# Turning the centroids earlier, and copying the fourth head on VectorE, in a fused clustered-attention and expert kernel

## The chip, the cores and the metric

One core of one Trainium2 chip. The metric is the time of the whole kernel on the device, in microseconds (us), lower is better. Places in a trace are us from the start of its span; the span is about 1.8 us shorter than the time.

Engine names in the profile: PE is TensorE's matmuls, PEld its weight loads, DVE is VectorE, ACT is ScalarE, POOL is GpSimd, SP is SyncE. L242 is line 242 of the kernel. In experiments that add or take lines, the same statement has a number a little higher or lower.

## The reference, cut to what matters

```python
# q, k, v: (4 batches, 8 heads, 768, 64) float32; centroids: (8 heads, 16, 64)
c_n = centroids / (norm(centroids) + 1e-06)
q_assign = argmax(einsum('bhsd,hcd->bhsc', q_n, c_n))     # 16 clusters a head
k_assign = argmax(einsum('bhsd,hcd->bhsc', k_n, c_n))
mask = q_assign[:, :, :, None] == k_assign[:, :, None, :]
attn_out = softmax(where(mask, q @ k.T / 8, -1e9)) @ v
# then, on the 3072 x 512 result: four experts, weighted by domain_probs
out = sum over e of  p[:, e] * (relu(x @ w1[e]) @ w2[e])
```

Keys and queries are first scored against the centroids of their head. Everything else waits for the first of these scores.

## The kernel before

In the trace of this kernel each engine runs the stretch below in the order of the statements: TensorE starts the twelve transposes of the keys from 4.63 to 6.42 us, that of the centroids at 6.53 and those of the queries from 6.81; ScalarE's four copies start from 5.54 to 6.82 and its cast at 7.20; VectorE lays out the centroids from 6.84 and copies the queries from 7.50. The first keys are turned (transposed) head by head on TensorE into PSUM and copied from there to SBUF (`all`, shown as tile `t`). The centroids are turned too and laid out block by block in `bdc`. A score is a matmul of `bdc` with the turned heads:

```python
def lay_centroids():
    pt = bank("misc")
    nc.tensor.matmul(pt[:, :128], cn2, ident, is_transpose=True)             # L185
    for r in range(2):
        dve(bdc[r * D:(r + 1) * D, :, r * CL:(r + 1) * CL],                  # L187
            pt[r * D:(r + 1) * D, :128].rearrange("p (h c) -> p h c", c=CL))
...
def turn(self, y, copy, shared=False):     # three transposes per head of the first keys
    ...
            nc.tensor.matmul(tp[:, c0:c0 + 128], raw[...], ident, is_transpose=True)   # L242
    ...
    copy(t32, tp[:, :m * w])                                                 # L252
...
def scores(self, copy):
    sc = self.bank()
    for j in range(HG):                    # four heads, four strips of 32 columns
        nc.tensor.matmul(sc[32 * j:32 * j + 32, :self.w], bdc[:, self.g * HG + j, :],
                         self.t32s[j // self.m][:, c0:c0 + self.w], ...)     # L267
    copy(self.scs[:, :self.w], sc[:, :self.w])                               # L271
...
for j in range(HG):                        # HG = 4
    k0.turn(j, act)                        # act: a copy on ScalarE
lay_centroids()
qa.turn(0, dve, True)                      # the first queries, copied by VectorE
k0.cast(0, 0, act)
k0.scores(act)
qa.scores(act)
```

Much later, in the experts, ScalarE applies the Relu that TensorE's second matmul reads.

```python
ht = moe.tile([128, 512], BF16, name="hT")
nc.scalar.activation(ht, ph, ACT.Relu)                                       # L745
...
nc.tensor.matmul(po, hT[f // per][:, c0:c0 + 128], W2[e][:, f, c], ...)      # L758
```

The softmax here doesn't subtract the row's maximum and nothing guards it: scores larger than these inputs give would overflow.

## Time and profile before

| | before |
|---|---|
| time, median of the first 3 runs | 472.22 us (472.22 to 472.25) |
| TensorE busy | 463.2 of 470.4 us |
| ScalarE, VectorE busy | 59%, 48% |
| key scores (L267) start, end | 7.58, 8.43 us |
| query scores (L267) start | 8.25 us |

TensorE is busy nearly throughout, so the time is its busy time plus the few gaps in it.

### The profile page before, as it was taken

What the parts mean: (1) busy time and instruction counts of PE and PEld (TensorE: products, weight loads), DVE (VectorE), ACT (ScalarE), POOL (GpSimd) and SP (SyncE); (2) the same over time, 40 slices, a digit from 0 to 9 for tenths busy, and PEclk for the clock granted to TensorE, in tenths of its full rate; (3) what the DMA queues carried; (4) which work ended last, traced back from release to release, by engine and by line L of the source; (5) the groups of instructions that cost most, each with busy time, mean ns of one, the idle gap of its engine ahead of it and who ended that gap; (6) DMA issues with size and microseconds to landing.
All of it is one profiled execution on the core that took longest, in us unless ns stands there. A gap on an engine that the chain in (4) does not pass through costs nothing.

```text
span 470.4 us, 11349 instructions
## 1 busy us (share of the span) xinstructions
PE 463.2 (98%) x4505; PEld 329.1 (70%) x4505; DVE 227.4 (48%) x554; ACT 276.9 (59%) x502; POOL 194.8 (41%) x301
## 2 busy tenths in 40 slices
PE   8999999999999999999999999999999999999996
PEld 5778777767767766777776667766766666667665
DVE  5964723542325563321234463523778767674112
ACT  5767675445655655566565656656665675664342
POOL 5936779275355593450433942000233232230000
PEclk9999999999999999999999999999999999999999
DMA  8999966996645941503666844220100100100101
GB/s 277 262 211 339 216 99 120 236 127 182 144 68 127 182 114 32 144 18 61 169 123 127 133 106 151 71 75 11 52 13 8 54 11 10 33 29 11 46 2 45
DMA packets 82381, 49.85 MB, mean 106 GB/s; under 512 B 57944, under 2 KB 77080, under 8 KB 82328
## 3 DMA queue, kind: packets, MB, share of 16 engines
q1 hardware_dynamic: 73080, 39.80, 35.1%
q0 software_dynamic: 8576, 9.25, 11.0%
q8 instruction: 35, 0.57, 0.5%
q14 instruction: 18, 0.15, 0.1%
q10 hardware_dynamic: 672, 0.08, 0.1%
HBM read 37.31 MB, written 6.30 MB: 93 GB/s over the span
## 4 chain that ended last, share of the span: by engine, by line
PE 95%; DVE 2%; DMA 1%; issue 0%; ACT 0%; SPq 0%; ACTq 0%
PE ps_mo L739 36%; PE ps_mo L758 35%; PE ps_s L649 9%; PE ps_av L676 7%; PE ps_s L562 1%; DMA kf<-oht 1%; PE ps_misc L562 1%; PE ps_s L87 1%; PE ps_mo L406 1%; PE ps_mo L242 1%; PE ps_misc L406 1%; DVE kf L315 1%; PE ps_misc L242 1%; PE ps_mo L267 0%; PE ps_misc L267 0%; DVE oh L287 0%
## 5 line engine op out<-in xcount | busy, mean ns | idle before, releaser
L655 ACT ACTIVATE at<-ps_s 128x512 bf16<-128x512 f32 x252 | 147.6, 596 | 115.5 <-PE ps_s L649 100.1
L739 PE MATMUL ps_mo<-xT,w1b 128*128 128x256 bf16 (+1 forms) x1664 | 195.9, 264 | 0.0
L758 PE MATMUL ps_mo<-w2b,hT 128*128 128x512 bf16 (+2 forms) x784 | 190.0, 375 | 0.0
L739 PEld LDWEIGHTS <-w1b 128*128 128x128 bf16 x1664 | 146.1, 98 | 24.8 <-issue 1.2
L745 ACT ACTIVATE hT<-ps_mo 128x512 bf16<-128x512 f32 x192 | 114.7, 598 | 60.5 <-PE ps_mo L739 57.7
L767 DVE SCALAR_TENSOR_TENSOR oacc<-ps_mo,psb,oacc 128x512 f32<-128x512 f32 (+1 forms) x74 | 54.3, 734 | 125.3 <-PE ps_mo L758 125.1
L758 PEld LDWEIGHTS <-hT 128*128 128x128 bf16 x784 | 66.9, 98 | 57.8 <-issue 3.1
L649 PE MATMUL ps_s<-qf,kf 80*128 80x256 bf16 (+1 forms) x456 | 82.7, 267 | 0.8 <-ACT at L655 0.4
L676 PEld LDWEIGHTS <-at 128*128 128x128 bf16 x1152 | 69.9, 97 | 15.3 <-issue 1.7
L676 PE MATMUL ps_av<-vx,at 128*128 128x65 bf16 x1152 | 80.3, 193 | 0.0
L662 POOL TENSOR_TENSOR at<-at,same 128x512 bf16<-128x512 bf16 x24 | 28.2, 1177 | 98.5 <-ACT at L655 83.0
L649 PEld LDWEIGHTS <-kf 80*128 80x128 bf16 x456 | 42.1, 98 | 20.6 <-issue 1.4
L380 POOL COPY t<-t 128x768 uint16<-128x768 uint16 x40 | 44.3, 1127 | 0.0
L579 DVE TENSOR_SCALAR same<-qf,late 128x256 bf16<-128x256 bf16 x144 | 39.0, 323 | 0.0
L662 DVE TENSOR_TENSOR at<-at,same 128x512 bf16<-128x512 bf16 x48 | 21.6, 450 | 25.9 <-ACT at L655 25.9
L364 POOL COPY h<-raw 128x768 uint16<-128x768 uint16 x24 | 20.3, 864 | 30.4 <-DMA raw<-in_k_dram 16.7
L361 POOL COPY h<-raw 128x768 uint16<-128x768 uint16 x16 | 13.1, 829 | 39.3 <-DMA raw<-in_q_dram 32.3
L765 DVE TENSOR_SCALAR oacc<-ps_mo,psb 128x512 f32<-128x512 f32 x18 | 13.5, 748 | 27.0 <-PE ps_mo L758 27.0
L683 DVE RECIPROCAL zr<-ps_av 128x4 f32<-128x4 f32 (+1 forms) x50 | 8.9, 178 | 33.3 <-PE ps_av L676 33.2
L336 POOL DMA_DIRECT2D qf<-oht x40 | 20.4, 519 | 7.5 <-DVE oht L313 3.9
L422 POOL COPY st<-sct 128x384 uint16<-128x384 uint16 x16 | 11.0, 736 | 28.8 <-DMA sct<-scs 28.8
L685 DVE TENSOR_TENSOR xn<-ps_av,zr 128x256 bf16<-128x256 f32 (+1 forms) x50 | 20.7, 414 | 1.7
(130 smaller groups left out, 263.2 us busy)
## 6 DMA issues: line engine op xcount, KB each, us to landing
raw<-in_v_dram SPq DMA_DIRECT2D x8, 768.0 KB, 5.4
out_dram<-oacc SPq DMA_DIRECT2D x23, 256.0 KB, 2.0
raw<-in_k_dram SPq DMA_DIRECT2D x7, 768.0 KB, 7.5
raw<-in_q_dram SPq DMA_DIRECT2D x6, 768.0 KB, 5.7
w1b<-in_moe_w_dram POOLq DMA_DIRECT2D x4, 1024.0 KB, 12.3
w2b<-in_moe_w_dram POOLq DMA_DIRECT2D x4, 1024.0 KB, 17.6
qf<-nos SPq DMA_DIRECT2D x2, 768.0 KB, 5.2
xT<-xn SPq DMA_TRANSPOSE x80, 2.4
```

Source lines behind the costliest of these rows:

```text
L336: (nc.gpsimd if self.b or self.i0 and self.g else nc.sync).dma_start(out=self.rows(slice(D, D + CL), j, r), in_=self.oht[p0:p0 + CL, :self.w])
L380: pool(self.all[:, y * w:(y + 1) * w].bitcast(U16)[:, z::2], self.t16[:, (2 * z + y) * w:(2 * z + y + 1) * w])
L579: nc.vector.tensor_scalar(same[:, x * 256:(x + 1) * 256], clusters(b)[:, g, w, k // 2, k % 2, :], key_nos[b % 2][:, g, 8 * i + 4 * (k // 2 ...
L649: nc.tensor.matmul(sp[:, x * n:(x + 1) * n], KF[b % 2][:K, h, r, i * 128:(i + 1) * 128], QF[b % 2][:K, h, rs[0]:rs[-1] + 1, w * 128:(w + 1 ...
L655: nc.scalar.activation(at, sp, ACT.Exp, scale=scale)
L662: (nc.gpsimd if n4 in POOL_STEPS else nc.vector).tensor_tensor(at, at, same_cluster(b, w, cur), op=ALU.mult)
L676: nc.tensor.matmul(av[:, h % 2, m, :], at[:, c0:c0 + 128], VX[b % 2][:, h, 2 * i + r, :], start=(first and x == 0 and m == 0), stop=(last ...
L685: nc.vector.tensor_tensor(xn[:, :nr].rearrange("p i j d -> p j i d"), av[:, :, :, :D], zr.broadcast_to([128, 2, nr, D]), op=ALU.mult)
L739: nc.tensor.matmul(ph[:, x * n:(x + 1) * n], W1[e][:, i, (f + x) * 128:(f + x + 1) * 128], xT[:, i, :], start=(i == 0), stop=(i == ND - 1))
L745: nc.scalar.activation(ht, ph, ACT.Relu)
L758: nc.tensor.matmul(po, hT[f // per][:, c0:c0 + 128], W2[e][:, f, c], start=(f == 0), stop=(f == NF - 1))
L767: nc.vector.scalar_tensor_tensor(oacc[:, c], po, pap, oacc[:, c], op0=ALU.mult, op1=ALU.add)
```

## The change

Its intent: the layout of the centroids should no longer come after everything else the first scores need, and ScalarE should no longer have four copies in a row ahead of them.

```diff
-    for j in range(HG):
+    for j in (0, 1):
         k0.turn(j, act)
     lay_centroids()
+    k0.turn(2, act)
+    k0.turn(3, dve)
     qa.turn(0, dve, True)
```

No instruction is added or removed in total. The centroid transpose takes TensorE's seventh place instead of the thirteenth, and one copy goes from ScalarE's stream to VectorE's.

## The prediction

> **What bounds the kernel now.** I read the page first (busy shares, slices), then the list of who waited for whom on TensorE, then the chain of waits in order of time, and last the timelines of TensorE, ScalarE and VectorE over the first eleven microseconds, because everything that the change touches happens there.
>
> From the page:
>
> ```profile
> PE 463.2 (98%) x4505; PEld 329.1 (70%) x4505; DVE 227.4 (48%) x554; ACT 276.9 (59%) x502; POOL 194.8 (41%) x301
> PE   8999999999999999999999999999999999999996
> PE 95%; DVE 2%; DMA 1%; issue 0%; ACT 0%; SPq 0%; ACTq 0%
> ```
>
> TensorE is busy for 463.2 of 470.4 us and carries 95% of the chain. The change alters none of its work (the same thirteen transposes, one of them in another place), so it can only take idle time away from it. All of the span outside its busy time is 7.2 us, and some of that is the start-up and the tail that nothing here touches. The waits of TensorE, longest first, are few:
>
> ```profile
> PE ps_misc L296 <- DVE oh L287: 0.6, 2, 0.4
> PE ps_s L649 <- ACT at L655: 0.4, 2, 0.3
> PE ps_mo L276 <- ACT scs L271: 0.4, 1, 0.4
> PE ps_s L649 <- DMA kf<-oht: 0.3, 1, 0.3
> PE ps_mo L296 <- DVE oh L287: 0.2, 1, 0.2
> ```
>
> Each column is the total, the count and the longest in us. They all lie in the first 28 us (the row for 60 to 470 us of the table by stretches shows no wait worth a line). So a head start won at the beginning reaches the end undiminished, if it survives every gate up to about 28 us; nothing later gives it back.
>
> Now the stretch that is edited. This is the chain of waits there (start, length, what):
>
> ```profile
> 4.79 1.58 PE ps_mo L242 x9
> 6.37 0.33 PE ps_s L242 x3
> 6.70 0.11 PE ps_misc L185
> 6.81 0.66 PE ps_av L242 x4
> 7.47 0.11 issue
> 7.58 0.95 PE ps_mo L267 x8
> 8.55 0.49 ACT scs L271
> 9.08 0.56 PE ps_mo L276 x3
> 9.66 0.56 DVE mx L284
> ```
>
> The reader should see the 0.11 us "issue" between 7.47 and 7.58: the scores of the first keys (L267) could have begun when the transposes of the queries ended, and something else held them. The timelines say what:
>
> ```profile
> 6.81 0.42 PEld L242 LDWEIGHTS ps_av<-ident,raw 128*128 128x128 f32 x4 [0.24 <-DMA raw<-in_q_dram]
> 6.82 0.50 ACT L252 COPY t<-ps_s 128x384 f32<-128x384 f32 x1
> 6.84 0.59 DVE L187 COPY bdc<-ps_misc 64x128 f32<-64x128 f32 x2 [1.26 <-PE ps_misc L185]
> 7.50 0.69 DVE L252 COPY t32q<-ps_av 128x512 f32<-128x512 f32 x1
> 7.55 0.19 PEld L267 LDWEIGHTS ps_mo<-t,bdc 128*32 128x32 f32 x8 [0.32 <-ACT t L252]
> 8.25 0.16 PEld L267 LDWEIGHTS ps_av<-t32q,bdc 128*32 128x32 f32 x8 [0.51 <-DVE t32q L252]
> ```
>
> Two things must be there for these scores: the fourth head's copy (ScalarE, 6.82 + 0.50 = 7.32) and the laid-out centroids (VectorE, 6.84 + 0.59 = 7.43). The list names ScalarE as releaser, but the centroids were ready 0.11 us after it. They, not the copy, were the later one.
>
> [...] at 59% and 48% neither is short of time, and both sit in front of L267. [...] The trace has 0.56 us (the L252 copy of a head on VectorE at 13.16) and 0.48 to 0.50 us, so VectorE is the slower place by some 0.06 to 0.08 us[...]. [...] transposes 0.21 us apart at about 5 us and 0.11 us apart after 6 us.
>
> **The change part by part.**
>
> 1. The centroid transpose (L185) goes from slot 13 of the thirteen transposes to slot 7. Its input is ready: the second scaling of the centroids ends at 5.06 + 0.25 = 5.31. Single transposes in the trace start at 6.10, 6.21, 6.31, 6.42 and 6.53 (slots 9 to 13), and slot 6 at 5.72, so slot 7 starts at about 5.88 and ends 0.27 later, at 6.15. VectorE, idle since 5.58, then copies the centroids from about 6.19 to 6.78 instead of 6.84 to 7.43. That gate opens 0.65 us earlier.
>
> 2. Heads three and four are transposed one slot later, 0.11 us. The third head's copy on ScalarE moves from 6.45 to about 6.56, and ends near 7.04. Nobody waits for that.
>
> 3. The fourth head's copy goes to VectorE. Its last transpose takes slot 13 and ends at 6.81, so the copy runs 6.84 + 0.56 = 7.40. On ScalarE it ended at 7.32. This gate gets 0.08 us later.
>
> 4. ScalarE loses 0.37 us of serial work (its copies start 0.37 us apart), and its first cast, from 7.20, starts near 6.9. Nothing on the chain reads that cast before 12.66.
>
> 5. The query copy on VectorE waits for the query transposes, and these for a DMA that lands at about 6.8, whatever stands before them on TensorE. It starts at 7.50 as before, since VectorE is free at 7.40. So the query scores still start at 8.25.
>
> Sum: the last input of the key scores was ready at 7.43 and will be at 7.40: 0.03 us. What may be added is the handover. From 7.43 to the weight load at 7.55 took 0.12 us, where other releases in this trace take 0.05 to 0.06 (the query copy ends at 8.19 and its load starts at 8.25). The first score matmul waited on two engines at once; after the change the build has it wait for inputs long present, and only the fourth for VectorE. The four heads use separate 32-column strips and run side by side (four start within 0.02 us, four second passes 0.32 us later), so the fourth alone sets the end. If its weights load at 7.40 + 0.06 = 7.46, the gain is 0.09 us. Total: 0.03 to 0.09 us.
>
> From there: ScalarE's score copy (8.55), the transpose back (9.08), max and one-hot on VectorE all move with it. The transposes of the next keys at 9.79 wait for a DMA and don't move, but the one-hot transpose waits 0.23 us behind them for VectorE, so up to about 0.2 us still passes. From 12.06 to 19 VectorE is the chain, nearly without gaps, and moves as a block. Then comes
>
> ```profile
> 20.01 4.60 DMA kf<-oht
> 24.75 0.22 PE ps_s L649
> ```
>
> a small transfer that lands 4.6 us after its issue, amid weight loads that keep all 16 queues full. TensorE waits 0.27 us for it. If its latency stays 4.6 us, the gain passes; its four copies took 4.6 to 4.8.
>
> My expectation is a gain of about 0.08 us, 472.22 to 472.14; I round to 472.1.
>
> **Rivals.**
>
> A: ScalarE was the true gate, as the releaser column says, with its four copies in a row. Then relieving it would free the scores by up to the end of the query transposes: their last starts at 7.20, so the scores could start at 7.31, a gain of 0.24 to 0.27 us, and 471.95. For it: the column. Against: the copy ended at 7.32, 0.23 us before the load, and in the new order the fourth head is on VectorE until 7.40, so even then the fourth strip can't start at 7.31.
>
> B: VectorE becomes the bound. Its 0.56 us copy stands ahead of the query copy; if it starts late (centroid copies behind a late L185)[...], the query copy and all after it slip by 0.1 to 0.2 us: 472.3 to 472.4. Against: VectorE is idle from 5.58, and there is 0.10 us between 7.40 and 7.50.
>
> C: the small transfer hides it: it lands when the full queues let it, not 4.6 us after its issue. Then the wait at 24.75 grows by what was won, and the time stays 472.2, or moves by its own scatter of 0.2 us either way.
>
> **Range and chances.** The central case is 472.1; A and C reach down to about 471.9, B and C up to 472.4. The three runs before differ by 0.03 us, but another session or chip may add a few tenths, so I take 471.7 to 472.5. A change of 2% is 9.4 us, more than all the idle time of TensorE, so faster by that is out of reach, and slower would need a new wait where I see none: faster 0.005, same 0.985, slower 0.01.
>
> **What would show it.** In the changed profile: the centroid copies end before 6.9 on VectorE; the fourth head's copy runs there at about 6.84 to 7.40; the weight loads of L267 for the fourth head at 7.46 to 7.55; ScalarE's score copy at 8.43 to 8.52; the one-hot transpose of 10.89 earlier by the same; the transfer of 20.01 likewise, and TensorE's step at 24.75. I am wrong if the score copy starts at 8.3 or before (rival A), if the query copy starts after 7.55 (B), or if the shift seen at 19 us is gone at 25 us (C).

## The result, and the profile after

| | before | after |
|---|---|---|
| median of 4 runs | 472.24 us (472.22 to 472.28) | 472.37 us (472.29 to 472.40) |

The ratio is 1.0002, with an interval of 0.9985 to 1.002: the same at 2%. (Ratios here are the mean time of one kernel's runs over that of the other's of the same rounds, so not quite the ratio of the medians quoted.) Still, all four runs of the changed kernel lie above all four of the kernel before, by 0.13 us in the median, where a gain of 0.08 was predicted.

The busy times after, from the page:

```profile
span 470.5 us, 11349 instructions
PE 463.2 (98%) x4505; PEld 328.6 (70%) x4505; DVE 227.9 (48%) x555; ACT 276.4 (59%) x501; POOL 194.4 (41%) x301
```

TensorE's busy time is unchanged; one instruction went from ACT (502 to 501) to DVE (554 to 555). The chain of waits at the start, after (start, length, what):

```profile
1.76 4.91 DMA raw<-in_q_dram
6.67 0.04 issue
6.72 0.66 PE ps_av L242 x4
7.38 0.90 PE ps_mo L267 x8
...
8.30 0.49 ACT scs L271
...
8.83 0.56 PE ps_mo L276 x3
...
9.42 0.56 DVE mx L284
```

and three lines of VectorE's timeline there:

```profile
5.59 0.59 DVE L187 COPY bdc<-ps_misc 64x128 f32<-64x128 f32 x2
6.57 0.56 DVE L252 COPY t<-ps_s 128x384 f32<-128x384 f32 x1 [0.39 <-PE ps_s L242]
7.41 0.69 DVE L252 COPY t32q<-ps_av 128x512 f32<-128x512 f32 x1 [0.28 <-PE ps_av L242]
```

The gap before the scores is gone, and the copy of the scores starts at 8.30 instead of 8.55. The chain now begins with the load of the first queries (landed 6.67), no longer with the transposes of the keys. So the start of this trace is 0.25 us earlier, which is more than predicted; the experiments show below that the clock did most of it. Down the line, the chain at 20 us:

```profile
19.76 4.67 DMA kf<-oht
24.43 0.14 issue
24.56 0.22 PE ps_s L649
```

24.56 instead of 24.75: the lead of 0.25 us became 0.19 in the small transfer (4.67 against 4.60 us). The transfer runs while the weights load: from 20.00 to 24.60 us of the kernel before, the packets of the weights' queue alone took 112.5% of the span of the 16 DMA engines. When TensorE's matmuls of both traces are set side by side in program order, the changed kernel is ahead by 0.191 us (median) from 45 to 95 us and **behind by 0.083 us** from 102 to 170, and it stays so to the end. Something takes 0.274 us at one place. The chain there, first the kernel before:

```profile
98.99 0.12 PE ps_av L676 x4
99.12 1.34 PE ps_mo L739 x24
100.46 0.89 PE ps_mo L758 x4
```

and after:

```profile
98.84 0.61 ACT at L655
99.44 0.30 issue
99.75 0.61 ACT hT L745
100.36 0.05 issue
100.40 1.04 PE ps_mo L758 x4
```

Before, TensorE runs through (but for about 0.02 us, see the account below). After, it waits for a Relu of ScalarE, and the Relu starts 0.30 us after the exponential in front of it, in a stretch that the view calls "issue": time in which the engine waited for nothing that the profile shows. In the kernel before, the same Relu starts 0.03 us after that exponential (99.627 to 99.658 us).

Counting the records of ScalarE's stream in order, from zero and with its event waits and DMA issues, gives a lead (places, start to end in us):

```
before                                     after
190  99.029- 99.627  exponential           189  98.838- 99.435  exponential
191  99.599- 99.616  wait for an event     190  99.408- 99.425  wait for an event
192  99.658-100.255  Relu                  191  99.749-100.346  Relu
```

The removed copy moved every later ScalarE instruction up by one place. Elsewhere too the changed kernel has stretches of 0.31 to 0.34 us, right after an event wait, in which ScalarE stands idle. They end at 175.36, 243.12 and 449.97 us, and these are places 319, 447 and 831: all, like 191, are 63 more than a multiple of 128. The kernel before has one such gap, at 313.26 us, place 575, again 63 more than a multiple of 128. This gave the theory to test:

- **Theory (fetch).** ScalarE's sequencer pays about 0.3 us once in 128 instructions (the name is my guess at the cause). It costs nothing where ScalarE waits for another engine anyway, as just ahead of place 191 before, where the exponential on place 190 waited 2.35 us for TensorE; and it costs TensorE 0.27 us where a Relu with no slack stands there.
- **Rivals.** The gap is chance; or it belongs to the fourth copy on VectorE or to the new timing of the first 30 us; or any extra ScalarE instruction helps.

### The profile page after: what moved, and what is told of

Same layout as the page of the kernel before. It is cut to its first block, busy times and chain, and to the rows that moved or that the text cites. A ratio compares the mean times of both kernels' runs of the same rounds, so it can differ in the third digit from the quotient of the medians.

```text
span 470.5 us, 11349 instructions
## 1 busy us (share of the span) xinstructions
PE 463.2 (98%) x4505; PEld 328.6 (70%) x4505; DVE 227.9 (48%) x555; ACT 276.4 (59%) x501; POOL 194.4 (41%) x301
## 4 chain that ended last, share of the span: by engine, by line
PE 94%; DVE 2%; DMA 2%; ACT 0%; issue 0%; SPq 0%; ACTq 0%
PE ps_mo L758 35%; PE ps_mo L739 35%; PE ps_s L649 9%; PE ps_av L676 7%; PE ps_s L562 1%; DMA raw<-in_q_dram 1%; DMA kf<-oht 1%; PE ps_misc L562 1%; PE ps_mo L406 1%; PE ps_misc L406 1%; DVE kf L315 1%; PE ps_misc L242 1%; PE ps_mo L267 0%; PE ps_misc L267 0%; DVE oh L287 0%; DVE mx L284 0%
## 5 line engine op out<-in xcount | busy, mean ns | idle before, releaser
L739 PE MATMUL ps_mo<-xT,w1b 128*128 128x256 bf16 (+1 forms) x1664 | 195.9, 264 | 0.0
L758 PE MATMUL ps_mo<-w2b,hT 128*128 128x512 bf16 (+2 forms) x784 | 190.0, 375 | 0.1
L739 PEld LDWEIGHTS <-w1b 128*128 128x128 bf16 x1664 | 146.1, 98 | 24.7 <-issue 1.2
L758 PEld LDWEIGHTS <-hT 128*128 128x128 bf16 x784 | 66.9, 98 | 58.1 <-issue 3.1
```

The costliest lines, as they stand in the source:

```text
L739: nc.tensor.matmul(ph[:, x * n:(x + 1) * n], W1[e][:, i, (f + x) * 128:(f + x + 1) * 128], xT[:, i, :], start=(i == 0), stop=(i == ND - 1))
```

## The experiments

In every trace I measured the same two things: TensorE's shift against the first trace of the kernel before, as the median from 45 to 95 us and from 102 to 170 us, and their difference, the step at 100.3 us.

### One instruction more, early (after_pad1, after_pad1_again)

```diff
     nc.scalar.activation(warm, blank[:, :1], ACT.Exp)
+    pad = consts.tile([128, 1], F32, name="pad")
+    for x in range(1):
+        nc.scalar.activation(pad[:, x:x + 1], blank[:, :1], ACT.Exp)
```

> The changed kernel with one more ScalarE instruction, a 128x1 exponential right after the warming one, in time where ScalarE idles. Fetch theory (ScalarE's sequencer pays some 0.3 us at every 128th instruction, at place 63 of each 128, and the change, by taking one instruction out, put a Relu that TensorE waits for on place 191): the extra instruction puts the stream back where it stood before the change, the 0.31 us gap before the Relu at 99.7 us is gone, TensorE keeps its lead of 0.19 us past 100 us, and the time is 472.05 to 472.15. Rival (the loss at 100 us is chance in a DMA or comes of the fourth copy on VectorE): the time stays at 472.3 to 472.4.

> after_pad1 once more, beside the changed kernel in the same job. Fetch theory: no gap at place 191, and 0.25 to 0.45 us below the changed kernel in the mean; with the first query load landing near 6.35 us, 471.6; near 6.7 us, 472.05 to 472.15.

Measured: medians 472.12 (471.62 to 472.80) and 472.19 us (471.52 to 472.61), ratio to the kernel before 0.9994 both times. The step at 100.3 us is 0.000 and 0.001 us; the Relu is on place 192, 0.03 us behind its exponential. The spread of single runs is wider than expected (below).

### The changed kernel again (again_after, third_after)

> The changed kernel unaltered. Fetch theory: the gap of about 0.3 us stands again before the same Relu (ScalarE instruction 191, near 99.7 us), and the time is 472.29 to 472.40. Chance: the gap is gone or elsewhere, and the time of the runs without it is near 472.1. Also to see when the full clock is granted (3.98 us in the first profile, against 5.81 in the kernel before), and when the scores of the first keys start then (7.30 us in the first).

> The changed kernel once more, beside after_pad1_again. Gap of about 0.31 us before the Relu on place 191; 472.3 to 472.4 with the query load landing near 6.7 us, 471.9 to 472.0 with it near 6.35 us.

Measured: medians 472.37 and 472.33 us. The gap is there both times, at place 191, and the step is 0.274 us both times. It is not chance. The profiled run of third_after had the query load at 6.72 us but 472.97 us in all: the full clock came only at 6.73 us, and of the small transfers near 20 us one took 5.08 us. The expectation named only the load.

### The extra instruction near the place, and past it (after_pad_near, after_pad_past)

Both are the changed kernel with one small instruction late in the stream:

```diff
+        76: lambda: nc.scalar.activation(pad, warm, ACT.Exp),   # near: just ahead of the exponential
         86: lay_late_constants,
```

and the same with 79 instead of 76, which lies behind the Relu.

> The changed kernel with one extra 128x1 ScalarE instruction put right before the exponential of about 98.8 us, so that nothing differs up to 96 us, and the Relu moves from place 191 to 192. Fetch theory: no gap before that Relu, the lead at 100.3 us is kept, and the time is 0.2 to 0.3 us below the changed kernel, 472.05 to 472.15. Rival (the timing of the first 30 us sets off the gap): gap and 472.35 as in the changed kernel.

> The same extra instruction, but ahead of the exponential of about 107 us, behind the Relu, which stays on place 191. Fetch theory: the gap of 0.31 us at 99.7 us stays, TensorE loses 0.27 us at 100.3, and the time is that of the changed kernel, 472.3 to 472.4. Rival (any extra instruction helps, or the later places 319, 447 and 831 cost the time): 472.05 to 472.15.

The chain of after_pad_near:

```profile
98.58 1.34 PE ps_mo L740 x24
99.92 0.24 PE ps_mo L759
100.16 0.05 issue
100.21 0.59 PE ps_mo L759 x2
```

and of after_pad_past:

```profile
98.92 0.60 ACT at L656
99.53 0.30 issue
99.83 0.61 ACT hT L746
100.44 0.05 issue
100.49 0.39 PE ps_mo L759
```

Step 0.000 and 0.274 us; medians 471.81 and 472.24 us. The two kernels have the same instructions up to 95 us, those of the changed kernel, so the copy on VectorE alone does not make the gap. In the past kernel the instruction is there and does not help. Nor is it the timing of the start: from 45 to 95 us TensorE is 0.106 us ahead of the first trace in after_pad_past, which has the gap, and 0.098 us ahead in before_pad1 (below), which has none. What counts is which instruction stands on the place. Both medians came out below their expectations (472.05 to 472.15 and 472.3 to 472.4); "The sum" comes back to this.

### One instruction fewer in the kernel before (before_less1, before_less1_pool)

To bring the gap into the old order, ScalarE must lose an instruction and nothing else change. I took the issue of the load of the domain probabilities away from it, first to SyncE, behind its first loads:

```diff
-    nc.scalar.dma_start(
-        out=dp, in_=moe_domain_probs...)
 ...                                        # behind the first loads of keys, queries and values
+    nc.sync.dma_start(
+        out=dp, in_=moe_domain_probs...)
```

and then, with `nc.gpsimd`, to GpSimd at step 15.

> The kernel before with one ScalarE instruction fewer: the load of the domain probabilities is issued by SyncE behind its first loads. Nothing in the edited stretch changes. Fetch theory: ScalarE has 852 instructions, the Relu near 99.7 us stands on place 191 and starts some 0.3 us late, TensorE is held at 100 us by 0.05 to 0.3 us (it had no slack there before), and the time is 472.3 to 472.55. Rival: 472.24 as before.

> The kernel before with one ScalarE instruction fewer, this time without crowding SyncE's queue: GpSimd issues the load of the domain probabilities at step 15, far ahead of its use. Fetch theory: ScalarE place 191 is the Relu near 99.7 us, it starts 0.31 us late, TensorE loses 0.25 to 0.29 us at 100.3 us, and the time is 472.4 to 472.6 where the kernel before has 472.2 to 472.3. Rival (the gap belongs to the fourth head's copy on VectorE or to chance): no gap, 472.2 to 472.3.

As times both are failures: 477.86 and 484.78 us. The load is 512 packets of 96 bytes (in the first traces of both kernels) and cost far more than I had allowed: in before_less1_pool it took 12.88 us to land, against 4.7 in the kernel before. In the first, the small transfer of 20 us landed after it, and TensorE waited; the table by stretches (stretch, its length, busy time and count of each engine, granted clock, DMA share, GB/s) shows this:

```profile
24.00:26.50 2.50, 0.33 (x5) 0.34 (x5) 0.36 (x3) 0.49 (x1) 1.58 (x3) 0.88 1.26 212
26.50:33.00 6.50, 6.41 (x73) 6.09 (x72) 3.33 (x14) 4.18 (x7) 0.00 (x0) 0.52 1.15 210
```

TensorE was without work from 24.03 to 26.20 us, and the clock was at half from 25.90 to 32.73 us. In the second, VectorE waited 8.2 us for the load itself, and the granted clock was 0.73 from 33 to 44 us, where TensorE was busy for 3.35 of 11 us. But the step can be read all the same, 70 us later: 0.274 us in both. The chain of before_less1_pool at the same Relu:

```profile
111.18 0.61 ACT at L656
111.79 0.30 issue
112.09 0.61 ACT hT L746
```

So the order of before, with one ScalarE instruction fewer, has the same gap of 0.30 us at the same place 191. The half of the expectation on the time is refuted by my own edit; the half on the gap is met.

### One more in the kernel before, and the kernel before itself (before_pad1, again_before)

The edit of after_pad1, on the kernel before, and no edit at all.

> A control: the kernel before with the same extra early ScalarE instruction as after_pad1. Fetch theory: place 191 is then the exponential of about 99 us, which waits for TensorE anyway, so nothing is exposed, and the time is that of the kernel before, 472.1 to 472.3. Rival (the extra instruction helps by itself, in the first microseconds): 0.2 us or more below the kernel before.

> The kernel before, unaltered, profiled once more, to see how much of the first comparison was the clock. In its first profile the full clock came at 5.81 us and the centroid transpose (the last of thirteen) ended at 6.81. If the clock comes before 5 us this time: centroids laid out near 7.3 us, key scores at 7.35 to 7.45 instead of 7.58. If it comes at 5.8 us or later: 7.58 again. In both: an event wait, not a Relu, on ScalarE place 191, no gap at 99.7 us, and 472.1 to 472.3.

Measured: no gap at the Relu, step 0.000 and -0.001 us, medians 472.67 (472.06 to 472.91) and 472.58 us (472.06 to 472.73). Place 191 of before_pad1 is the exponential that waits for TensorE (2.35 us in the first trace of the kernel before), so by the theory the 0.3 us are hidden. An extra instruction does not help by itself. Both medians missed high, and again_before says what that is worth: the same kernel had 472.58 and, as the comparison of the same job, 472.20 us. A median of five can be off by 0.4 us, so the steps in the traces decide here, not the medians.

### The halves of the change (only_order, only_copy)

```diff
 # only_order                              # only_copy
+    for j in (0, 1):                     +    for j in range(3):
+        k0.turn(j, act)                  +        k0.turn(j, act)
+    lay_centroids()                      +    k0.turn(3, dve)
+    for j in (2, 3):                          lay_centroids()
+        k0.turn(j, act)
```

> Only the first half of the change: centroids turned after the second head, all four heads still copied by ScalarE, so that ScalarE keeps its 853 instructions. Fetch theory with the centroids as the gate: the scores start at 7.3 to 7.5 us instead of 7.58, no gap at 99.7 us, and the time is 472.0 to 472.15, below both kernels. If the fourth copy on ScalarE was the gate (rival A of the prediction): the scores start at 7.5 us or later and the time is 472.2 to 472.3.

> Only the second half of the change: VectorE copies the fourth head, the centroids stay behind all four heads. VectorE then copies the head first (0.56 us) and lays out the centroids after it, so the layout ends near 7.8 us instead of 7.2 to 7.4, the scores of the first keys start near 7.85 to 8.0, and the query copy starts near 7.9 instead of 7.5: 0.35 to 0.5 us lost at the start. ScalarE has 852 instructions, so the gap before the Relu on place 191 costs 0.27 us more. Together 472.8 to 473.1. If the small transfer of about 20 us hides the loss at the start: 472.5. If ScalarE's four copies in a row were what held the scores: 472.3 or less.

Measured: 472.21 us (472.00 to 472.60; expected were at most 472.15) with step 0.000, and 472.85 us (472.68 to 473.32) with step 0.273. In only_copy VectorE's two layouts end at 7.73 us, behind the head's copy, and the chain has them as the gate:

```profile
7.14 0.27 DVE bdc L187
7.42 0.01 issue
7.43 0.30 DVE bdc L187
7.74 0.14 issue
7.87 0.89 PE ps_mo L267 x8
```

In only_order the centroids are early, and ScalarE's fourth copy is the last input (ends 7.59 us, in a run whose clock came late):

```profile
6.32 0.59 DVE L187 COPY bdc<-ps_misc 64x128 f32<-64x128 f32 x2 [0.86 <-PE ps_misc L185]
7.11 0.48 ACT L252 COPY t<-ps_s 128x384 f32<-128x384 f32 x1
7.39 0.39 PEld L267 LDWEIGHTS ps_mo<-t,bdc 128*32 128x32 f32 x8 [0.17 <-ACT t L252]
```

In after_pad_past, with the clock equally late, VectorE's copy stands in that place and ends at the same time:

```profile
7.04 0.56 DVE L253 COPY t<-ps_s 128x384 f32<-128x384 f32 x1
7.36 0.42 PEld L268 LDWEIGHTS ps_mo<-t,bdc 128*32 128x32 f32 x8 [0.17 <-ACT t L253]
```

To compare starts, the clock has to be taken out: in the first trace of the kernel before, transposes start 0.21 us apart at about 5 us, ahead of the full clock at 5.81, and 0.11 us apart after it. The table has, for each profiled run, when the full clock was granted, when the query load landed, when the last of the thirteen transposes ended and when the key scores ended (us, from the traces):

| run | full clock | load landed | 13th transpose | scores end | behind the 13th | behind the load |
|---|---|---|---|---|---|---|
| before | 5.81 | 6.77 | 6.81 | 8.43 | 1.62 | 1.66 |
| again_before | 4.40 | 6.61 | 6.59 | 8.21 | 1.62 | 1.60 |
| before_pad1 | 5.81 | 6.33 | 6.77 | 8.39 | 1.62 | 2.06 |
| only_order | 6.33 | 6.59 | 7.02 | 8.48 | 1.46 | 1.89 |
| only_copy | 4.17 | 6.80 | 6.74 | 8.72 | 1.98 | 1.92 |
| after_pad_past | 6.28 | 6.31 | 7.00 | 8.48 | 1.48 | 2.17 |
| third_after | 6.73 | 6.72 | 7.22 | 8.70 | 1.48 | 1.98 |
| after | 3.98 | 6.67 | 6.54 | 8.16 | 1.62 | 1.49 |
| again_after | 4.96 | 6.67 | 6.48 | 8.15 | 1.67 | 1.48 |
| after_pad1 | 5.03 | 6.36 | 6.39 | 7.87 | 1.48 | 1.51 |
| after_pad_near | 4.19 | 6.35 | 6.31 | 7.83 | 1.52 | 1.48 |
| after_pad1_again | 4.81 | 6.32 | 6.28 | 7.80 | 1.52 | 1.48 |

In the old order the scores end 1.62 us behind the thirteenth transpose, with the full clock granted at 4.40 us as at 5.81. In the new order they end 1.48 us behind the later of transposes and load. So the change is worth 0.14 us at the start, at most. The order alone gives it (1.46 in only_order); the copy on VectorE adds nothing, and without the new order it costs 0.36 (1.98 against 1.62). only_order and only_copy are one trace each, and the times are too coarse to show 0.14: the mean of only_order was 472.29 us, that of the kernel before in the same job 472.35.

Where the load lands after the transposes, the gain is smaller, and in the first changed trace there is hardly any: with its thirteenth transpose (6.54) the old order would have ended its scores at about 6.54 + 1.62 = 8.16 us, by this estimate the very time measured. The kernel before with an early clock (again_before) says the same: its score copy starts at 8.33 us, against 8.30 in the first changed trace. So nearly all of the 0.27 us that the first two profiles show at this place (8.43 to 8.16) is the clock, granted at 3.98 us in one and at 5.81 in the other.

### The sum

The steps, all runs together:

| ScalarE's place 191 | runs | step at 100.3 us |
|---|---|---|
| the Relu | after, again_after, third_after, after_pad_past, only_copy, before_less1, before_less1_pool | 0.273 to 0.274 |
| something else | again_before, before_pad1, only_order, after_pad1, after_pad1_again, after_pad_near | -0.001 to 0.001 |

Over all fourteen traces ScalarE stands idle for 0.31 to 0.34 us right after an event wait 34 times, and each time at a place 63 more than a multiple of 128. A gap of 0.285 us (at 378.95 us in the first changed trace), in contrast, moves with its instruction (places 697 to 699).

The 0.27 us are lost in every trace with the Relu on this place. What the start wins is between 0 and 0.14 us, and it passes a small transfer that scatters by 0.3 us. So that 0.14 won and 0.27 lost make just the 0.13 us of the medians is partly luck: the sum fits, but no run tests it that finely.

The changed kernel with one more ScalarE instruction (after_pad1, after_pad_near, after_pad1_again) had the lowest mean in each of the three jobs: 472.09, 471.93 and 472.08 us; the kernel before had 472.35, 472.25 and 472.35 beside it, and the changed kernel (or after_pad_past, with the same gap) 472.55, 472.29 and 472.45. The 0.3 us over the kernel before are more than the 0.14 that the start explains, and each job's own interval (0.9981 to 1.0007 taken together) takes in 1. There is also a rival for the rest. In all five traces with the extra tile `pad` the query load landed at 6.31 to 6.36 us, in the seven others that left the loads alone at 6.59 to 6.80, and this within each job. The edit that adds the instruction also adds a tile, and no run has the tile without the instruction; whether the tile makes the loads faster is open. The steps at 100.3 us don't depend on it: after_pad_near and after_pad_past both have the tile.

**What stays open.** What the sequencer does at these places is argued, not shown. For it being a fetch of instructions speaks that in the changed kernel's first trace a packet of 8192 bytes of the instruction queue starts 0.65 to 0.9 us after each of the four gaps (at 100.65, 176.16, 243.78 and 450.62 us). In each of the seven runs with the gap such a packet starts 0.65 to 1.32 us after the Relu; in the seven without it, none starts between 98 us and the Relu or in the 3 us after it. No run shows how many instructions such a packet holds.

## Why the prediction was right or wrong, point by point

The time, 472.37, lies in the range, and the chances put nearly all on "within 2%". The sign of the small gain was wrong. That the time fell into the range is partly luck: it was made 0.8 us wide for sessions, chips and the rivals named, not for a loss of this kind.

- **The bound**: right on TensorE's busy time, the same 463.2 us. Wrong is "So a head start won at the beginning reaches the end undiminished, if it survives every gate up to about 28 us; nothing later gives it back." This is the step that failed. I had looked at waits that exist in the kernel before (my list left out the longest, 1.2 us at the very start, and one of 0.3 us at 26.7 us; neither matters here). The one that gave the lead back was new as a wait, and TensorE had no slack there: already in the kernel before the weight load of L758 starts 0.05 us after the end of that Relu (100.26 to 100.31), and its first matmul 0.07 us behind the last L739, where 0.056 is the usual distance. A wait of about 0.02 us appears in no list. In its place the runs showed a loss of 0.274 us at 100.3 us.
- **Part 4** counted the copy taken from ScalarE as 0.37 us of free time and found that "Nothing on the chain reads that cast before 12.66". It left out that taking one instruction out moves all later ones of that stream by one place.
- **Parts 1 to 3**: right in mechanism. The centroids were the gate (only_order gets the whole gain without the copy), and the copy is no better on VectorE. The size was off: the sum was 0.03 to 0.09 us, and 1.62 against 1.48 makes it 0.14. The mis-sized term is the handover. I took the 0.12 us from the layout's end to the first weight load, but the fourth strip's matmul started at 7.60, 0.17 behind it; in after_pad_past it starts 0.06 us behind VectorE's copy (7.59 to 7.65). (The copy of a head took 0.56 us on VectorE and 0.48 to 0.50 on ScalarE in the first trace of the kernel before; these went into the sum.)
- **Part 5**: right. The load of the queries landed at 6.31 to 6.80 us in all runs but the two that moved another load, and it is the gate in four of the five traces of the new order with a clock before 5.1 us.
- **Rival A** (ScalarE's copies): refuted by only_order, which keeps the four copies in a row and has the whole gain, though its sign in the profile came true. I had written that a score copy at 8.3 or before would show it, and it started at 8.30. The early clock made that (8.33 in again_before, without any change); a sign has to be compared at the same clock.
- **Rival B** (VectorE as the bound): not seen in the changed kernel; in only_copy it is what happens.
- **Rival C** (the small transfer): partly true as scatter. It took 4.52 to 4.83 us where it was the gate of the head's first block. In again_before the send went out 0.21 us earlier than in the first trace, and TensorE went on at the same time all the same:

```profile
19.80 4.83 DMA kf<-oht
24.63 0.14 issue
24.76 0.22 PE ps_s L649
```

## What to carry to other kernels

Taking an instruction out of an engine's stream is not local: it moves all later instructions of this engine by one place, and here, where ScalarE stood idle for 0.30 us on place 191, it put another instruction on that place and cost TensorE 0.274 us. When a change moves the time by a few tenths of a microsecond, set the bottleneck engine's instructions of both traces side by side in order and look for the steps; waits hidden by hundredths of a microsecond are in no list. And compare starts at the same clock, or relative to an event that carries the clock in it, before crediting a change with what the clock did.

## What the runs measured of the hardware

- ScalarE stands idle for 0.31 to 0.34 us right after an event wait at places 63 more than a multiple of 128 (34 of 34), and with the Relu at 99.7 us on such a place TensorE lost 0.273 to 0.274 us in seven of seven runs. That the gap is a fetch of instructions is my reading.
- In the fourteen profiles here the full clock came at 3.93 to 6.73 us, with the first matmul at 1.19 us in each trace compared: a scatter of 2.8 us.
- In before_less1 TensorE stood idle from 24.03 us, and the clock was at half from 25.90 to 32.73 us: in this run it fell 1.9 us after TensorE's last work.
- A small SBUF to SBUF transfer of 12 KB near 20 us, while the weights were loading, took 4.5 to 5.1 us from issue to landing in the twelve runs that left the loads alone.
